# Fewer bank marks, a later third banded set and lean first-pass quads in a gated attention-and-mixer kernel

## The chip, the cores and the metric

One core of one Trainium2 chip. The metric is the device time of one execution, in microseconds (us), and lower is better. A kernel is compared only with the runs of the kernel before in the same rounds on the same chip.

## The reference, cut to what matters

Two branches work on the same x (2048 rows of 1024 columns), and a gate mixes them.

```python
g = sigmoid((x * gate_w).sum(-1, keepdims=True))
# a: attention over 8 positions, two apart (32 heads of 32)
qkv = x @ wqkv                               # banded q.k products, softmax over 8, weighted sum of v
a = o @ wo
# b: gated mixer
z = gelu(x @ w_in)                           # z1: 1792 columns, z2: 1792 columns
z2 = layernorm(z2)
b = (z1 * (w_sp @ z2 + b_sp)) @ w_out
out = g * a + (1 - g) * b
```

## The kernel before

TensorE does all products. Most large ones are done in "quads": a Strassen-like scheme that makes four output blocks from seven products instead of eight. A quad uses four PSUM banks, X, Y, Z and V. Its intermediate sums stay in PSUM: a copy or an addition by another engine puts one bank's content into another, and the next product adds onto it. Two quads run interleaved, one on banks 0 to 3 and one on banks 4 to 7.

```python
def chain(..., put, share, N, lean=False, ...):      # the quad of z2 and z1
    X, Y, Z, V = bank_roles[side]
    bank_roles[side] = [X, V, Y, Z] if lean else [Y, V, X, Z]
    product(X, pairs(A11, B11), True, N)
    last_seed[0] = nc.scalar.copy(Y[:, n], X[:, n])
    yield
    product(V, pairs(S1, T1), True, N)               # share: vs <- V
    ...
    product(Y, pairs(S2, T2), False, N)
    plus(Z, Y)                                       # VectorE: Z = Y + vs
    yield
    product(X, pairs(A12, B21), False, N)
    put(0, 0, X)                                     # ScalarE: gelu
    yield
    product(Y, pairs(S3, T3), False, N)
    if not lean:
        seed = nc.scalar.copy(X[:, n], Y[:, n])      # a bank of its own for the last block
    inst = plus(V, Y)
    if not lean:                                     # one reader of a bank at a time
        tc.add_manual_dep(inst.ins, seed.ins.name, SYNC, ...)
    put(1, 1, V)
    yield
    product(Z, pairs(S4, B22), False, N)
    put(0, 1, Z)
    yield
    W = Y if lean else X
    product(W, pairs(A22, T4), False, N)
    put(1, 0, W)
```

The kernel is built on the rule that a product adds onto what another engine wrote only where an earlier product has marked the bank. The kernel makes such marks with products whose results are thrown away:

```python
def mark(bs, N=512, lo=0):
    for b in bs:
        pe((N - lo) / 2400.0)                        # the planner's clock, see below
        nc.tensor.matmul(b[:, lo:N], xT[:, 4, 0:P], xT[:, 4, 0:N - lo], start=(lo == 0), stop=True, ...)
```

The attention's q.k products ("banded sets", three for each of eight groups of heads) use banks 4 to 7 as well. ScalarE casts each set into a staging buffer, and transfers store it from there to DRAM. The first set of a group has a buffer of its own, the second and third share two in turn. Later transfers load the sets back, rearranged, as the logits that VectorE works on.

```python
def group_tiles(g):                                  # the order of TensorE's work in group g
    ...                                              # tiles: the q and k products of the next group
    return [tiles[0], band[0], tiles[1], band[1], tiles[2], band[2]] + tiles[3:]
```

Between 60 and 280 us the order of VectorE's attention work and of all transfers is not written down. A planner decides it while the program is built: it keeps a modelled clock for each engine (`pe(dur)`, `act(...)`, `dve(...)`) and issues a transfer or an attention operation when its turn comes on those clocks. In this stretch the transfers go out on one queue, SP's, in that order.

```python
play(main[0:8 - (not g)])
if g == 2:                                           # the v quads, in the middle of group 2
    mark(banks[4:8])
    for i in range(0, 8, 2):
        run(v_quad(i), v_quad(i + 1), step=step)     # step: let the planner issue what is due
...
mark(banks[4:8], ZC)                                 # before the z2 quads (ZC = 448 columns)
...
mark(banks, 512, ZC)                                 # before z1, the columns 448 to 511
```

The z2 quads run in two passes; only the second is lean (`LEAN = (False, True)`).

## Time and profile before

673.67 us, median of three runs (673.57 to 673.83).

From the page of the kernel before, its first two parts' totals and the chain of waits by engine:

```profile
span 673.4 us, 10760 instructions
## 1 busy us (share of the span) xinstructions
PE 661.3 (98%) x4193; PEld 316.9 (47%) x4193; DVE 449.8 (67%) x663; ACT 296.8 (44%) x627; POOL 6.9 (1%) x15
...
PE 86%; ACT 5%; DVE 5%; DMA 2%; issue 1%; SPq 0%; POOL 0%; ACTq 0%; DVEq 0%
```

PE (TensorE) is the bound. What it can lose is gaps between products, and products that compute nothing. The timeline of TensorE alone shows both. Its columns are start, duration, engine, line, operation and shapes, the count, and in brackets the idle time before and what ended it. L288 are q and k tiles, L350 banded sets, L576 marks, L808 z2 tiles, L431 the products of quads.

```profile
83.14 0.64 PE L350 MATMUL psum_all<-arena 32*64 32x71 bf16 x56 [0.23 <-ACT arena L358]
...
87.18 1.03 PE L576 MATMUL psum_all<-arena 128*128 128x512 bf16 x4
88.05 30.59 PE L431 MATMUL psum_all<-arena 128*128 128x320 bf16 x224
118.67 7.07 PE L288 MATMUL psum_all<-arena 128*128 128x512 bf16 x32
...
162.00 0.64 PE L350 MATMUL psum_all<-arena 32*64 32x71 bf16 x56 [0.47 <-ACT arena L358]
...
195.96 0.92 PE L576 MATMUL psum_all<-arena 128*128 128x448 bf16 x4 [0.38 <-ACT arena L358]
196.72 12.41 PE L431 MATMUL psum_all<-arena 128*128 128x448 bf16 x64
209.38 1.67 PE L431 MATMUL psum_all<-arena 128*128 128x448 f16 x8 [0.25 <-ACT arena L801]
211.39 3.19 PE L431 MATMUL psum_all<-arena 128*128 128x448 f16 x16 [0.33 <-ACT psum_all L504]
214.94 3.94 PE L431 MATMUL psum_all<-arena 128*128 128x448 f16 x20 [0.36 <-DVE psum_all L492]
219.29 7.05 PE L431 MATMUL psum_all<-arena 128*128 128x448 bf16 x36 [0.40 <-ACT psum_all L526]
226.89 11.07 PE L431 MATMUL psum_all<-arena 128*128 128x448 f16 x56 [0.55 <-DVE psum_all L492]
238.27 42.58 PE L431 MATMUL psum_all<-arena 128*128 128x448 f16 x220 [0.31 <-DVE psum_all L492]
280.68 0.19 PE L576 MATMUL psum_all<-arena 128*128 128x64 bf16 x1
281.64 0.36 PE L576 MATMUL psum_all<-arena 128*128 128x64 bf16 x7 [0.77 <-ACT arena L801]
281.84 252.98 PE L431 MATMUL psum_all<-arena 128*128 128x512 bf16 x1168
535.03 135.10 PE L431 MATMUL psum_all<-arena 128*128 128x512 f16 x624 [0.21 <-DVE arena L1123]
```

Read it from the top: banded sets wait for ScalarE's cast of the set before (L358); three places carry marks (L576); the first z2 pass (196.7 to 238.3 us) has six gaps, the second pass (to 280.7 us) none that is listed; and from 282 us TensorE runs without a listed gap to the output stage at 535 us.

### The profile page before, as it was taken

Reading aid. Unit: us, or ns where it says so; the run is one execution under the profiler, and the core shown is the slowest. Engines: PE = TensorE matmul, PEld = TensorE weight load, DVE = VectorE, ACT = ScalarE, POOL = GpSimd, SP = SyncE. Lnnn points to the kernel's source line nnn. Section 1 sums busy time; section 2 is a strip of 40 time slices with the busy share of each in tenths; the row PEclk is TensorE's granted clock in tenths of the full one; section 3 lists DMA queues with packets and bytes.
Section 4 is the critical chain, followed back from the end, with each engine's and each line's share of the span. In section 5 each row is a group of like instructions: output and inputs, shape, how many; then the busy total and the mean of one; then the engine's idle time right before and its main releaser. Section 6 shows DMA issues by size and latency. Waiting matters only on the chain.

```text
span 673.4 us, 10760 instructions
## 1 busy us (share of the span) xinstructions
PE 661.3 (98%) x4193; PEld 316.9 (47%) x4193; DVE 449.8 (67%) x663; ACT 296.8 (44%) x627; POOL 6.9 (1%) x15
## 2 busy tenths in 40 slices
PE   8999999999999999999999999999999999999998
PEld 4544467444444445444444444444444444444443
DVE  2520699957997999897679676887766685333301
ACT  3354676556578767697854212112112112222221
POOL 1000000000000000001000000000000000000000
PEclk9999999999999999999999999999999999999999
DMA  9988554777476041359983477557356398954100
GB/s 228 167 209 225 116 121 125 210 193 198 95 200 175 1 125 29 94 149 219 234 211 134 99 174 175 139 146 235 102 139 167 87 192 189 202 121 101 44 31 32
DMA packets 235684, 98.17 MB, mean 146 GB/s; under 512 B 189792, under 2 KB 221936, under 8 KB 235632
## 3 DMA queue, kind: packets, MB, share of 16 engines
q1 hardware_dynamic: 234944, 97.01, 59.2%
q8 instruction: 33, 0.54, 0.4%
q10 hardware_dynamic: 688, 0.46, 0.2%
q14 instruction: 19, 0.16, 0.1%
HBM read 45.10 MB, written 36.61 MB: 121 GB/s over the span
## 4 chain that ended last, share of the span: by engine, by line
PE 86%; ACT 5%; DVE 5%; DMA 2%; issue 1%; SPq 0%; POOL 0%; ACTq 0%; DVEq 0%
PE psum_all L431 67%; PE psum_all L288 14%; PE psum_all L298 3%; ACT arena L358 2%; PE psum_all L350 1%; DVE psum_all L492 1%; ACT arena L801 1%; DMA band_d<-arena 1%; DVE arena L977 1%; DMA att_L<-band_d 1%; DVE arena L698 1%; PE psum_all L313 1%; DMA arena<-o_d 0%; PE psum_all L576 0%; ACT arena L291 0%
## 5 line engine op out<-in xcount | busy, mean ns | idle before, releaser
L431 PE MATMUL psum_all<-arena 128*128 128x512 f16 (+5 forms) x2436 | 500.1, 367 | 2.9 <-DVE psum_all L492 1.2
L431 PEld LDWEIGHTS <-arena 128*128 128x128 f16 (+1 forms) x2436 | 238.2, 98 | 264.2 <-issue 7.9
L288 PE MATMUL psum_all<-arena 128*128 128x512 bf16 x512 | 114.9, 379 | 0.9 <-ACT gl_s L301 0.8
L288 PEld LDWEIGHTS <-arena 128*128 128x128 bf16 x512 | 48.5, 98 | 57.7 <-issue 2.1
L694 DVE TENSOR_TENSOR arena<-arena,att_A 128x2048 f16<-128x2048 bf16 (+1 forms) x44 | 73.5, 1704 | 0.3
L291 ACT CAST arena<-psum_all 128x512 bf16<-128x512 f32 x64 | 37.3, 586 | 49.2 <-PE psum_all L288 49.2
L567 DVE TENSOR_TENSOR arena<-arena 128x1024 f16<-128x1024 f16 (+3 forms) x36 | 20.6, 582 | 47.6 <-PE psum_all L431 26.7
L449 ACT COPY psum_all<-psum_all 128x512 f32<-128x512 f32 (+1 forms) x30 | 15.8, 527 | 79.0 <-PE psum_all L431 78.2
L492 DVE TENSOR_TENSOR psum_all<-psum_all,arena 128x448 f32<-128x448 f32 (+1 forms) x58 | 37.2, 660 | 9.1 <-PE psum_all L431 5.2
L801 ACT ACTIVATE arena<-psum_all 128x448 bf16<-128x448 f32 x64 | 34.1, 546 | 19.1 <-DVE psum_all L492 11.2
L569 DVE TENSOR_TENSOR arena<-arena 128x1024 f16<-128x1024 f16 (+3 forms) x36 | 20.6, 580 | 29.3 <-PE psum_all L431 12.5
L1044 ACT ACTIVATE arena<-psum_all 128x512 bf16<-128x512 f32 x56 | 30.9, 595 | 18.2 <-PE psum_all L431 12.1
L698 DVE TENSOR_TENSOR arena<-arena 128x2048 f16<-128x2048 f16 (+1 forms) x22 | 37.2, 1703 | 0.1
L470 ACT COPY psum_all<-psum_all 128x512 f32<-128x512 f32 (+1 forms) x30 | 15.9, 529 | 46.2 <-PE psum_all L431 45.1
L358 ACT CAST arena<-psum_all 128x1988 f16<-128x1988 f32 (+3 forms) x25 | 33.9, 1357 | 5.0 <-DMA band_d<-arena 2.5
L460 ACT COPY psum_all<-psum_all 128x512 f32<-128x512 f32 (+1 forms) x30 | 15.7, 527 | 40.5 <-PE psum_all L431 40.0
L455 ACT COPY arena<-psum_all 128x512 f32<-128x512 f32 (+1 forms) x30 | 16.2, 543 | 35.3 <-PE psum_all L431 30.2
L851 ACT ACTIVATE arena<-arena 128x896 bf16<-128x896 bf16 x32 | 30.0, 943 | 0.0
L568 DVE TENSOR_TENSOR arena<-arena 128x1024 f16<-128x1024 f16 (+3 forms) x36 | 20.6, 582 | 8.2 <-PE psum_all L431 7.9
L1230 DVE TENSOR_TENSOR arena<-psum_all,arena 128x512 bf16<-128x512 f32 x8 | 5.5, 690 | 29.0 <-ACT psum_all L470 29.0
L298 PE MATMUL psum_all<-arena 128*128 128x385 bf16 x128 | 22.6, 327 | 0.3 <-DVE arena L321 0.3
L657 DVE TENSOR_TENSOR att_m<-att_L 128x256 f16<-128x256 f16 x8 | 2.3, 288 | 29.4 <-DMA att_L<-band_d 29.3
(89 smaller groups left out, 414.0 us busy)
## 6 DMA issues: line engine op xcount, KB each, us to landing
arena<-v_d SPq DMA_DIRECT2D x8, 960.0 KB, 6.5
z_d<-arena SPq DMA_DIRECT2D x14, 512.0 KB, 3.7
arena<-z_d SPq DMA_DIRECT2D x14, 512.0 KB, 4.3
zg_d<-arena SPq DMA_DIRECT2D x56, 128.0 KB, 2.2
arena<-zg_d SPq DMA_DIRECT2D x32, 224.0 KB, 3.1
band_d<-arena SPq DMA_DIRECT2D x28, 248.5 KB, 4.7
arena<-in_A_wqkv_dram SPq DMA_DIRECT2D x16, 256.0 KB, 4.4
o_d<-arena SPq DMA_DIRECT2D x4, 1024.0 KB, 6.1
```

The lines of the kernel that those rows point to most:

```text
L288: nc.tensor.matmul(ps[:], w[:, t, kt, :], xT[:, kt, 512 * c:512 * (c + 1)], start=(kt == 0), stop=(kt == KT - 1))
L291: nc.scalar.copy(dst[:, :, 256 * c:256 * (c + 1)], ps[:].rearrange("p (n e) -> p e n", e=2))
L298: nc.tensor.matmul(ps[:, 0:VP + 1], xT[:, kt, i * P:(i + 1) * P], wvp[:, kt, :], start=(kt == 0), stop=(kt == KT - 1))
L358: nc.scalar.copy(dst, src)
L431: nc.tensor.matmul(bank[:, 0:N], lhsT, rhs, start=(start and m == 0), stop=(m == n - 1), skip_group_check=True)
L492: last_add[0] = nc.vector.tensor_tensor(out[:, n], a[:, n], vs, ALU.add)
L567: first = nc.vector.tensor_tensor(s_out[0], a21, a22, ALU.add)
L694: lambda ws=ws, in0=in0, in1=in1: tt(p5[:, ws], in0[:, ws], in1[:, ws], ALU.mult)), False
L698: lambda a=p3[:, ws], b=p3[:, ws.start + 4:ws.stop + 4]: tt(a, a, b, ALU.add)), not n
L801: nc.scalar.activation(z2[:, i + 8 * a, ZC * c:ZC * (c + 1)], bank[:, 0:ZC], ACT.Gelu_apprx_tanh, accum_out=s1[:, 4 * n + c:4 * n + c + 1])
L851: return nc.scalar.activation(junk, src, ACT.Square, accum_out=(s2, s2h)[x][:, n:n + 1])
L1044: last_gelu[0] = nc.scalar.activation(z1s[:, f, a, :], bank[:], ACT.Gelu_apprx_tanh)
```

## The change

Its intent is to take small gaps and empty products from TensorE. Three parts:

- *Lean.* In the first z2 pass too, the last block is added onto Y, so the copy from Y to X and its ordering are not needed.
- *Bands.* The third banded set of a group comes one tile later, so that the cast of the second has two tiles' time.
- *Marks.* Only the banks that a quad needs marked (Y and Z; X and V are started afresh) are marked, and later, behind the quad's first product. At z1 the Y banks are still marked ahead of it, and the Z banks before the third products.

```diff
-    LEAN = (False, True)
+    LEAN = (True, True)
@@ group_tiles
+        if g + 1 < NG:
+            return [tiles[0], band[0], tiles[1], band[1], tiles[2], tiles[3], band[2]] + tiles[4:]
         return [tiles[0], band[0], tiles[1], band[1], tiles[2], band[2]] + tiles[3:]
@@ behind_first(n): at the first step of a pair of quads, mark(banks[5:7], n)   (cut)
@@ before the v quads
-            mark(banks[4:8])
             for i in range(0, 8, 2):
-                run(v_quad(i), v_quad(i + 1), step=step)
+                run(v_quad(i), v_quad(i + 1), step=behind_first(VH) if i == 0 else step)
@@ before the z2 quads
-    mark(banks[4:8], ZC)
@@ quad_step
+            if n == 0 and count[0] == 0:
+                mark(banks[5:7], ZC)
@@ before z1
-    mark(banks, 512, ZC)
+    mark([b[1] for b in bank_roles], 512, ZC)
@@ in the first pair of z1 quads, before its third products
+    mark([b[2] for b in bank_roles], 512, ZC)     # (simplified)
```

## The prediction

> **What bounds it now.** TensorE. On the page PE is 661.3 of 673.4 us (98%); the chain of waits is 86% PE; the granted clock is 1.00. The Trainium skill, "Perfetto Trace Analysis", section "Identifying the Most-Contended Engine", warns that matmul busy share does not show distance to roofline, so I count what PE can lose: gaps, and matmuls that compute nothing. PE's busy time per stretch shows about 12 us of gaps, 3 at startup and 3 at the end, both untouched; from 300 to 600 us under 0.5 us. So the change works between 60 and 300 us, where VectorE (DVE) is mostly over 90% busy.
>
> **What the change does.**
>
> 1. *Third banded set a tile later* (six groups, not the last). The banded products reuse four banks that ScalarE empties in 1.81 us after a 0.58 us tile copy; one tile of 1.72 us does not cover that. The timeline shows waits for that cast of 0.23, 0.47 and 0.29 us at 83, 162 and 178 us and 0.10 and 0.14 elsewhere. Two tiles cover it: -1.2 us. The 0.35 us at 193 stays.
> 2. *Marks.* Before the v quads four 512-wide matmuls become two of 320: 0.85 to 0.27 us, -0.6. Before the z2 quads four of 448 become two, behind the first product: -0.37, and most of a 0.38 us wait for the last banded cast goes: -0.7 in all. At z1 eight 64-wide ones become two and two, and the 0.77 us wait for a gelu at 280.7 goes, since the banks marked first are emptied earlier: -0.9. (Copies by VectorE and ScalarE do not set the bits that make a matmul add: "PSUM — Partial Sum Buffer", "The four PSUM rules"; no trace here shows the bits.)
> 3. *Lean z2 quads in the first pass.* Seven ScalarE copies of 0.54 us go, and with them 2.9 us of DVE waits for them. The last product now waits for DVE's addition, three products (2.3 us) behind. Between 196.7 and 238.3 us PE has 2.2 us of gaps (0.25 gelu, 0.33 seed copy, 0.40 removed copy, and 0.36, 0.55, 0.31 for additions); the second pass, already lean, has none over 0.2. I expect 1.4 back.
>
> **What comes back.** DVE is nearly full from 196 to 300 us and its work does not shrink. The instruction order shows two attention operations of 1.22 us pushed behind z1's start; PE may lead by that plus recovered DVE idle time. In the second quad pair DVE still sits behind the load of the last group's logits (1.94 us idle at 205). I allow 0.8 us of new waits there or in early z1.
>
> **Sum.** 1.2 + 0.6 + 0.7 + 0.9 + 1.4 - 0.8 = 4.0 us on PE's critical path: 673.67 to 669.6 us. Range 668.2 to 671.8. Faster by over 2%: 1%; within 2%: 98%; slower by over 2%: 1%.
>
> **What would show it.** No wait for the banded cast before the last group; z2 quads start about 2.5 us earlier; gaps in the first z2 pass fall from 2.2 to about 1; z1 starts about 4 us earlier with no gelu wait; after 300 us the lead stays constant. Wrong: PE's waits for additions grow, or the lead shrinks after 300 us.
>
> **What would make it wrong.** DVE's order comes from a planner with modelled clocks; if additions sit behind a 2.28 us attention operation or the logits' load, PE waits at the last product of a lean quad and up to 2 us come back.

## The result

670.95 us, median of four runs (669.78 to 672.09), against 673.69 us (673.57 to 673.83, four runs). The ratio is 0.9959, with a 95% interval of 0.9935 to 0.9983. The four runs fall into two pairs, 669.8 and 672.05 us, with granted clocks of 0.997 to 1.000; the profile is of one of the faster pair.

The page of the changed kernel:

```profile
span 668.0 us, 10729 instructions
...
PE 657.8 (98%) x4185; PEld 315.7 (47%) x4185; DVE 448.9 (67%) x663; ACT 293.1 (44%) x620; POOL 6.8 (1%) x15
...
PE 88%; DVE 7%; DMA 2%; SPq 1%; issue 1%; ACT 0%; DVEq 0%
```

TensorE is busy 3.5 us less and the span is 5.4 us shorter. ScalarE's share of the chain has gone from 5% to nothing, and VectorE's has grown from 5 to 7%. The removed copies explain little of that: in the chain before, the casts of the banded sets (L358) are 2.5%, the gelus (L801) 1.3%, and the removed copies (L526) 1.3 us, or 0.2%. SPq is the sequencer that issues the transfers, and it is now 1% of the chain.

The timeline of TensorE alone of the changed kernel, in the same columns as before:

```profile
85.89 0.71 PE L431 MATMUL psum_all<-arena 128*128 128x320 bf16 x4
86.43 0.43 PE L576 MATMUL psum_all<-arena 128*128 128x320 bf16 x2
86.70 30.05 PE L431 MATMUL psum_all<-arena 128*128 128x320 bf16 x220
116.78 7.07 PE L288 MATMUL psum_all<-arena 128*128 128x512 bf16 x32
...
157.10 0.64 PE L350 MATMUL psum_all<-arena 32*64 32x71 bf16 x56 [0.25 <-ACT arena L358]
...
161.80 0.64 PE L350 MATMUL psum_all<-arena 32*64 32x71 bf16 x56 [0.50 <-ACT arena L358]
...
193.87 0.54 PE L576 MATMUL psum_all<-arena 128*128 128x448 bf16 x2
194.25 5.46 PE L431 MATMUL psum_all<-arena 128*128 128x448 bf16 x28
200.39 71.61 PE L431 MATMUL psum_all<-arena 128*128 128x448 f16 x376 [0.69 <-DVE psum_all L492]
272.23 2.58 PE L431 MATMUL psum_all<-arena 128*128 128x448 f16 x12 [0.23 <-DVE psum_all L492]
274.65 0.22 PE L576 MATMUL psum_all<-arena 128*128 128x64 bf16 x2
274.71 3.62 PE L431 MATMUL psum_all<-arena 128*128 128x512 bf16 x16
...
306.55 221.63 PE L431 MATMUL psum_all<-arena 128*128 128x512 f16 x1024 [0.54 <-DVE psum_all L492]
529.59 135.10 PE L431 MATMUL psum_all<-arena 128*128 128x512 f16 x624 [1.41 <-DVE arena L1136]
```

The marks are smaller and sit behind the first products, as intended, and the gelu wait at z1 is gone. The first z2 pass has one gap left instead of six. But two waits for the banded cast are still there, at 157 and 162 us, and three waits later on are new or larger: 0.23 us at the end of the second z2 pass (272.2), 0.54 us at 306.6 and 1.41 us at the output stage (529.6, before 0.21).

The lead of the changed kernel at the same point of TensorE's program, worked out from such lines of the two timelines (start before minus start after):

| point | lead, us | gained in the stage | predicted |
|---|---|---|---|
| q and k tiles at 48.0 us, ahead of all changed code | 0.8 | 0.8 | 0 |
| end of the v quads (118.67, 116.78) | 1.9 | 1.1 | 1.8 for the bands and these marks, |
| ahead of the z2 quads | 2.3 | 0.4 | these two rows together |
| behind the z2 marks | 3.2 | 0.9 | 0.7 |
| z1 marks (280.68, 274.65) | 6.0 | 2.8 | 1.4 |
| z1's products behind them (281.84, 274.71) | 7.1 | 1.1 | 0.9 |
| output stage (535.03, 529.59) | 5.4 | -1.7 | -0.8 somewhere |
| end of the span (673.4, 668.0) | 5.4 | 0 | 0 |

This table is of one of the faster executions, which is 3.9 us below the median of before; the median gain of all four is 2.7 us. So the predicted total held, but it was not made up of the predicted terms. The first 0.8 us is chance: no instruction ahead of that point differs. The z2 passes gave twice what was predicted. The bands and the first marks gave 1.5 of 1.8, and 1.7 us was lost late.

*Why the z2 passes gave more.* The gaps listed in a TensorE timeline are too short, because a matmul's record is longer than the matmul's spacing. In the changed kernel 376 matmuls of 448 columns took 71.61 us, that is 0.1905 us each (0.190 from start to start, as the 71.61 includes the last record's overhang), while their records average 352 ns. The last record ahead of a stall therefore covers about 0.16 us of it. From start to start the account is different. Before, the six stretches from 196.72 to 238.27 us hold 200 matmuls in 41.55 us. They need 38.10, so 3.45 us were lost, while the listed gaps add up to 2.20. After, 28 matmuls take 6.14 us from 194.25 to 200.39 and need 5.33, so 0.81 was lost, and no gap is listed behind that in this pass. The difference is 2.64 us, against 1.51 by listed gaps (2.20 less 0.69).

### The profile page after: what moved, and what is told of

Same layout as the page of the kernel before. It is cut to its first block, busy times and chain, and to the rows that moved or that the text cites. A ratio compares the mean times of both kernels' runs of the same rounds, so it can differ in the third digit from the quotient of the medians.

```text
span 668.0 us, 10729 instructions
## 1 busy us (share of the span) xinstructions
PE 657.8 (98%) x4185; PEld 315.7 (47%) x4185; DVE 448.9 (67%) x663; ACT 293.1 (44%) x620; POOL 6.8 (1%) x15
## 4 chain that ended last, share of the span: by engine, by line
PE 88%; DVE 7%; DMA 2%; SPq 1%; issue 1%; ACT 0%; DVEq 0%
PE psum_all L431 71%; PE psum_all L288 12%; PE psum_all L298 3%; DVE arena L694 3%; DMA band_d<-arena 1%; PE psum_all L350 1%; DVE arena L698 1%; SPq L186 1%; PE psum_all L313 1%; DMA arena<-o_d 1%; DVE arena L699 1%; DVE psum_all L492 0%; DVE arena L703 0%; DMA att_L<-band_d 0%; ACT arena L300 0%
## 5 line engine op out<-in xcount | busy, mean ns | idle before, releaser
L567 DVE TENSOR_TENSOR arena<-arena 128x1024 f16<-128x1024 f16 (+3 forms) x36 | 20.7, 584 | 53.4 <-PE psum_all L431 26.7
L801 ACT ACTIVATE arena<-psum_all 128x448 bf16<-128x448 f32 x64 | 34.1, 545 | 19.8 <-DVE psum_all L492 10.8
L569 DVE TENSOR_TENSOR arena<-arena 128x1024 f16<-128x1024 f16 (+3 forms) x36 | 20.6, 582 | 26.8 <-PE psum_all L431 12.1
L358 ACT CAST arena<-psum_all 128x1988 f16<-128x1988 f32 (+3 forms) x25 | 33.9, 1356 | 4.8 <-DMA band_d<-arena 2.7
L568 DVE TENSOR_TENSOR arena<-arena 128x1024 f16<-128x1024 f16 (+3 forms) x36 | 20.6, 583 | 8.1 <-PE psum_all L431 7.9
L570 DVE TENSOR_TENSOR arena<-arena 128x1024 f16<-128x1024 f16 (+3 forms) x36 | 20.4, 580 | 1.7 <-PE psum_all L431 1.6
```

The source lines that it names most:

```text
L358: nc.scalar.copy(dst, src)
L567: first = nc.vector.tensor_tensor(s_out[0], a21, a22, ALU.add)
L801: nc.scalar.activation(z2[:, i + 8 * a, ZC * c:ZC * (c + 1)], bank[:, 0:ZC], ACT.Gelu_apprx_tanh, accum_out=s1[:, 4 * n + c:4 * n + c + 1])
```

## The experiments

The texts name theories by letters. P is the prediction's account, in which the parts have the worths that can be read in the trace. D is its rival in the first set, in which the changed kernel has two levels of time. S, formed after the first set, and O in the third set hold that the order in which the planner issues its work decides. Twelve runs were made in three sets, each set on one chip of its own. All twelve gave correct results. The medians of the kernel before in the same rounds were 674.63 us (673.26 to 675.90) in set 1, 674.85 (673.77 to 676.80) in set 2 and 675.44 (673.64 to 676.91) in set 3.

| run | set | median us (range) | ratio to before [95%] | waits for the banded cast, us |
|---|---|---|---|---|
| a1_again: the changed kernel | 1 | 671.23 (668.61-673.23) | 0.9949 [0.9927, 0.9971] | 1.0 |
| l1_lean_only | 1 | 671.79 (671.31-672.36) | 0.9957 [0.9943, 0.9971] | 1.5 |
| b1_bands_only | 1 | 673.06 (672.54-677.46) | 0.9986 [0.9963, 1.0009] | 0 |
| m1_marks_only | 1 | 676.05 (673.55-677.63) | 1.0017 [0.9998, 1.0036] | 4.3 |
| m2_marks_clock_kept | 2 | 673.15 (672.62-674.26) | 0.9970 [0.9955, 0.9985] | 0.4 |
| u1_after_no_bands | 2 | 671.82 (670.79-673.22) | 0.9954 [0.9937, 0.9971] | 2.4 |
| k1_after_clock_kept | 2 | 668.64 (668.60-669.56) | 0.9909 [0.9894, 0.9924] | 0 |
| b0_before_again: one profile | 2 | 674.24, state unknown | - | 1.0 |
| a2_third: the changed kernel | 3 | 672.60 (670.54-673.47) | 0.9958 [0.9941, 0.9974] | 2.3 |
| k3_kept_no_bands | 3 | 671.54 (670.67-675.69) | 0.9960 [0.9936, 0.9984] | 1.3 |
| k4_kept_no_lean | 3 | 672.07 (670.66-673.65) | 0.9953 [0.9937, 0.9970] | 0 |
| k2_kept_late_sums | 3 | 669.27 (667.95-670.80) | 0.9910 [0.9893, 0.9926] | 0 |

The last column is what the view of waits of each run's one profile gives for TensorE's listed waits for the cast at L358 between 60 and 186 us; waits too short for that view are not in it. In the profiles of before and after it is 1.0 and 0.7.

### Set 1: the parts alone

**The changed kernel again.** No edit.

> The changed kernel again. Its four times lay at 669.8 and 672.05, two each. Theory D: the 2.2 us between them come from when transfers land (the load of the last stage's first rows, for which the changed kernel waited 1.4 us at 529.6 us even in its fast profile, or the stores of the bands at 154 to 162 us); then the new runs fall at the same two levels, about half each, and never between. Rival C: a matter of the chip; then all runs of one chip fall at one level. Granted clock stays 0.997 to 1.00 either way.

It ran from 668.6 to 673.2 us. That is neither one level nor two: the two pairs of the first result were chance, and D's two levels fall. On this chip the kernel before spreads by 2.6 us as well.

**Lean alone.**

```diff
-    LEAN = (False, True)
+    LEAN = (True, True)
```

> Only the lean quads. Theory P (the parts add up as read from the trace of after, where the lead over the kernel before grew by 2.7 to 2.8 us in the z2 passes): 2 to 2.8 us faster than before, 670.9 to 671.7. Rival M (removed waits move to the next reuse of a bank, only all parts together pay): under 1 us faster. Gaps of PE between 196.7 and 238 us fall from 2.2 to under 1 us.

It is 0.43% faster, 2.9 us of 674.63 (2.0 to 3.8 by the interval). That agrees with the account from start to start (2.64) and not with the predicted 1.4. Its profile keeps one gap in the first pass, 0.96 us for an addition at 207.70 us, ahead of the last product of a lean quad, where the prediction looked for one.

**Bands alone.** Only the new branch of `group_tiles`.

```diff
+        if g + 1 < NG:
+            return [tiles[0], band[0], tiles[1], band[1], tiles[2], tiles[3], band[2]] + tiles[4:]
```

> Only the third banded set a tile later. Theory P: the lead of after grew 0.9 us over the six groups, so 0.5 to 1.0 us faster, 672.7 to 673.2. Rival M: same as before within 0.3 us, the later bands being paid back in the attention's chain or at the marks before the v quads.

It is 0.14% faster, 0.9 us, and the interval includes no gain at all. Its profile has no wait for the cast up to 186 us. Two tiles do cover the cast, here.

**Marks alone.** The whole third part, without the other two.

```diff
-            mark(banks[4:8])
-                run(v_quad(i), v_quad(i + 1), step=step)
+                run(v_quad(i), v_quad(i + 1), step=behind_first(VH) if i == 0 else step)
-    mark(banks[4:8], ZC)
+            if n == 0 and count[0] == 0:
+                mark(banks[5:7], ZC)
-    mark(banks, 512, ZC)
+    mark([b[1] for b in bank_roles], 512, ZC)     # and b[2] later, as in the change
```

> Only the marks. Theory P: 0.6 at the v quads, 0.7 to 0.9 at z2, 0.9 to 1.1 at z1, together 2.0 to 2.6 us faster, 671.1 to 671.7. Rival M: only the 1.0 us of matmuls removed, 672.7.

Both theories missed this. TensorE has less to do, and the kernel is not faster; the measured ratio is 1.0017. From TensorE's timeline of this run, the second 56-matmul banded set of three successive groups:

```profile
145.47 0.64 PE L350 MATMUL psum_all<-arena 32*64 32x71 bf16 x56 [0.73 <-ACT arena L358]
...
162.73 0.64 PE L350 MATMUL psum_all<-arena 32*64 32x71 bf16 x56 [1.70 <-ACT arena L358]
...
179.69 0.64 PE L350 MATMUL psum_all<-arena 32*64 32x71 bf16 x56 [1.41 <-ACT arena L358]
```

In the profile of before no wait at these sets was over 0.47 us. And from the timeline of all engines of the same run, the cast that the middle one waits for:

```profile
160.86 1.82 ACT L358 CAST arena<-psum_all 128x1988 f16<-128x1988 f32 x1 [1.62 <-DMA band_d<-arena]
```

The cast is no longer than before (1.82 us), but ScalarE stood idle for 1.62 us ahead of it, waiting for a transfer: the store that empties the staging buffer the cast writes into. So the bound at this place is not ScalarE's time, as the prediction had it, but when the stores of the banded sets come due and land.

What had changed for them? A mark calls `pe(...)`, so a smaller mark also advances the planner's modelled clock by less. Around the v quads that is 4 x 512 - 2 x 320 = 1408 columns at 2400 a microsecond: 0.587 us. The planner then issues transfers and VectorE's work in another order. This is theory S.

### Set 2: the clock kept

**Marks alone, with the planner's clock as before.**

```diff
+            pe(4 * 512 / 2400.0 - 2 * VH / 2400.0)   # ahead of the v quads; no instruction
+    pe(2 * ZC / 2400.0)                              # ahead of the z2 quads
```

> The marks alone again, TensorE's instructions as in the marks-only kernel (which came out 0.17% slower than before), but the planner's clock is advanced by what the removed marks took, so that up to z1 the transfers and VectorE's work are issued in the order of the kernel before. Theory S (the marks are worth 2.0 to 2.6 us; the marks-only kernel lost them because the shifted planner reordered the stores of the bands among the weight loads, and ScalarE's casts, and then TensorE, waited for those stores: 3.8 us of waits at 145, 163 and 180 us): 1.5 to 2.5 us faster than before, and the three waits are back at 0.1, 0.5 and 0.3 us. Rival W (marks are worth nothing, whatever comes earlier waits at the next reuse): within 0.5 us of before or slower, as marks-only was.

TensorE's instructions are the same as in the marks-only kernel. Up to z1, transfers and VectorE's work stand in the order of the kernel before. It is 0.30% faster than before, 2.0 us, and its interval does not touch that of marks alone. The predicted 2.2 us for the marks was right, but only with the order kept.

**The changed kernel without the bands.**

```diff
-        if g + 1 < NG:
-            return [tiles[0], band[0], tiles[1], band[1], tiles[2], tiles[3], band[2]] + tiles[4:]
```

> The changed kernel with the third banded set back in its old place (lean quads and marks kept). Theory S: the move of the set is also what shields TensorE from late stores of the bands, so undoing it costs 2.5 to 4 us against the changed kernel (waits for the cast of 0.7 to 1.7 us in the groups from 140 to 180 us return): about 0 to 1.5 us faster than before. Rival A (parts simply add): undoing it costs the 0.9 us that bands-only gained, so 2.0 to 2.5 us faster than before.

I had expected that the later third set is what shields the changed kernel from the reordered stores, so that this one would gain only 0 to 1.5 us. It gained 0.46%, 3.1 us, about as much as the changed kernel itself. The waits for the cast did grow, to 2.4 us, but the time did not show it. The shield as I had it is not borne out. In the profiles, this kernel lacks what the later set brings further on (the waits at 272.2 and 306.6, see the end of Set 3), and its wait at the output stage is 0.19 instead of 1.41 us.

**The changed kernel with the planner's clock kept.** One line, ahead of the v quads; TensorE's instructions are unchanged.

```diff
+            pe(4 * 512 / 2400.0 - 2 * VH / 2400.0)
             for i in range(0, 8, 2):
```

> The changed kernel with the planner's clock advanced at the v quads as above; the transfers of groups 3 to 6 are then ordered as in bands-only, whose profile shows no wait for the cast there. Theory S: the waits of 0.25 and 0.50 us (0.97 us in the second profile of after) at 157 to 163 us go, 0.7 to 1.2 us faster than the changed kernel, 0.6 to 0.7% faster than before. Rival: those waits stay, being a matter of when the memory serves the stores, and the time is that of the changed kernel.

It is 0.91% faster than before, 6.1 us: more than either theory expected, so the waits at 157 to 163 us are not all that the order cost. The three ratios of the changed kernel are 0.9949, 0.9958 and 0.9959, and no interval of these reaches down to this one's upper end of 0.9924. So the changed kernel loses 0.40 to 0.50% to the order, 2.7 to 3.4 us. A sum check: lean alone (2.9), bands alone (0.9) and marks with the clock kept (2.0) make 5.8 us.

The cost of the order is shown in two pairs of kernels with the same instructions on TensorE: this one (0.40 to 0.50%) and marks alone without and with the clock kept (0.47%). A third pair does not show it: the changed kernel without the bands is at 0.9954 without and, in Set 3, at 0.9960 with the clock kept. The intervals leave room for a gain of about 0.23% at most there.

From the timeline of the changed kernel, issues on the transfer queue (SPq) and VectorE's first operation on the loaded logits:

```profile
128.79 0.60 SPq L186 DMA_DIRECT2D o_d<-arena  x1
129.44 2.03 SPq L186 DMA_DIRECT2D arena<-v_d  x1
...
148.20 1.28 SPq L186 DMA_DIRECT2D att_L<-band_d  x2
...
152.87 0.29 DVE L657 TENSOR_TENSOR att_m<-att_L 128x256 f16<-128x256 f16 x1 [8.15 <-DMA att_L<-band_d]
```

And from the same view of the changed kernel with the clock kept:

```profile
124.25 0.61 SPq L186 DMA_DIRECT2D o_d<-arena  x1
...
129.60 0.58 SPq L186 DMA_DIRECT2D arena<-v_d  x1
...
145.10 1.28 SPq L186 DMA_DIRECT2D att_L<-band_d  x2
...
149.75 0.29 DVE L657 TENSOR_TENSOR att_m<-att_L 128x256 f16<-128x256 f16 x1 [7.84 <-DMA att_L<-band_d]
```

The same logits are asked for 3.1 us later in the changed kernel, although its v quads had started 0.3 us earlier (85.89 against 86.17). The store of o has moved behind two stores of banded sets and two weight loads. The load of v keeps its place and its time. In this profile the chain of waits of the changed kernel leads from there to TensorE's remaining gap; its columns are start, duration and what ran:

```profile
154.35 7.28 DMA band_d<-arena
161.65 2.44 DMA att_L<-band_d
...
197.51 2.28 DVE arena L694
199.79 0.56 DVE psum_all L492
200.39 5.64 PE psum_all L431 x29
```

A store of a banded set takes 7.28 us to land, the load of the logits follows it, VectorE works through its attention operations without a break of note, and the addition that TensorE waits for at 200.39 comes at their end. With the clock kept, TensorE's timeline has no gap in this pass:

```profile
193.66 76.83 PE L431 MATMUL psum_all<-arena 128*128 128x448 bf16 x404
```

That does not show that the order makes this gap, however. In the kernel of Set 3 with late sums, whose transfers and VectorE's work stand in the order of the kernel with the clock kept up to 520 us, the gap is there:

```profile
200.91 71.61 PE L431 MATMUL psum_all<-arena 128*128 128x448 f16 x376 [0.65 <-DVE psum_all L492]
```

And the changed kernel's third profile has none. The gap at this product stands in seven of the ten profiles with new marks (0.65 to 1.35 us) and in none of the four with the old ones, lean or not. So it goes with the new marks rather than with the order; how it comes about is not shown.

The two profiles differ by 1.2 us at the end only (668.0 and 666.8), since the changed kernel was profiled in one of its faster executions.

**The kernel before, one look.**

> The kernel before, profiled again, to see what moves from run to run without any change. Expected: the waits that begin with a transfer (first block of x, stores of the bands, rows of the last stage) differ by up to 1 us from its first profile; waits between engines alone (seeds, additions, gelus) are the same to 0.1 us.

Most of its waits repeat those of the first profile: 1.0 us for the cast, 0.18 us at the output stage, and four of the six gaps of the first z2 pass to 0.01 us. The other two, 0.25 us for a gelu and 0.33 us for a seed copy, are gone, so not all waits between engines are the same to 0.1 us. Up to the last of these gaps the pass takes 40.71 us here against 41.55, so the account from start to start carries that much chance.

### Set 3: what the order costs, and to whom

**The changed kernel a third time.** No edit.

> The changed kernel a third time, to stand on one chip beside the clock-kept variants below. Theory O (the planner's order of transfers is what the changed kernel loses against its clock-kept sister): 0.4 to 0.6% faster than before, its profile again with waits of 0.7 to 1 us for the cast between 150 and 165 us and 0.7 to 1.4 us for the first additions of the z2 quads. Rival H (the 0.91% of the clock-kept kernel was the chip's doing): 0.8 to 0.9% here too.

The ratio repeats. The profile caught a slower execution (672.95 us), with one wait of 2.34 us for the cast at 164.02, behind a cast that stood idle 4.01 us for the store of a banded set. The view by stretches of this run shows what it cost beyond itself; its columns are the stretch, its length, the busy time of PE, PEld, DVE, ACT and POOL with counts, the granted TensorE clock, the DMA share and GB/s:

```profile
164.00:166.00 2.00, 1.98 (x60) 1.08 (x60) 0.83 (x1) 2.00 (x3) 0.00 (x0) 0.50 0.73 92
166.00:168.00 2.00, 2.00 (x8) 0.81 (x7) 1.63 (x5) 1.12 (x2) 0.00 (x0) 0.67 0.81 189
168.00:170.00 2.00, 2.00 (x11) 0.91 (x10) 1.97 (x3) 1.01 (x3) 0.00 (x0) 1.00 0.84 222
```

The granted clock was 0.50 in the 2 us behind the stall and 0.67 in the mean of the next 2. The 40 tile products that follow took 10.09 us, against 8.81 in the faster profile. So a stall of 2.34 us cost about 3.6. Such a stall can account for part of the spread of the changed kernel's times. No wait for an addition in z2 came with it, which the expectation had named.

**The clock kept, without the bands.** Against the changed kernel:

```diff
+            pe(4 * 512 / 2400.0 - 2 * VH / 2400.0)
-        if g + 1 < NG:
-            return [tiles[0], band[0], tiles[1], band[1], tiles[2], tiles[3], band[2]] + tiles[4:]
```

> Lean quads and marks with the clock kept, the third banded set in its old place. Theory O with parts that add once the order is right (lean 2.9, marks 2.0, bands 0.9 us alone): 4.5 to 5.2 us faster than before, 0.67 to 0.77%. If instead the later set is the main shield against late stores, under 3.5 us faster, with waits over 0.7 us for the cast in the groups from 140 to 180 us.

It gained 0.40%, 2.7 us, less than expected, and 0.51% less than with the bands. So the bands are worth 3.4 us here and 0.9 alone. By the table's intervals these are 1.5 to 5.3 and -0.6 to 2.5 us, which overlap, so it is not shown that the parts fail to add; two of this kernel's six runs (673.42 and 675.69) pull its mean up. The waits in one profile (1.3 us) do not explain 3.4 us.

**The clock kept, the first pass not lean.** Against the changed kernel:

```diff
+            pe(4 * 512 / 2400.0 - 2 * VH / 2400.0)
-    LEAN = (True, True)
+    LEAN = (False, True)
```

> Bands and marks with the clock kept, the first z2 pass not lean. Adding parts: 2.7 to 3.5 us faster than before (0.40 to 0.52%), and the first z2 pass shows waits for the removed copies and the additions again, 1.5 to 2.3 us of them between the start of the z2 quads and the second pass. If lean is worth only the 1.4 us predicted, 4.5 us or more faster.

It gained 0.47%, as expected. The lean part is worth 0.44% here, 3.0 us, the same as alone.

**The clock kept, and the output stage's first sums behind the last addition of the spatial quads.** This was aimed at the wait of 1.41 us at the output stage. Against the changed kernel with the clock kept:

```diff
+            first = sums4(...)                       # the attention-row part of output quad 0
+            if i == 0 and k0:
+                tc.add_manual_dep(first.ins, wait_for[0].ins.name, NOSYNC, ...)
```

> The clock-kept kernel, with the sums for the first output quad that wait for the attention's rows placed behind the last spatial quad's additions on VectorE (the scheduler also moves some of TensorE's products there). If the wait at the start of the output stage (0.5 to 1.5 us at 528 to 530 us in four of six profiles of kernels with new marks) is these sums standing ahead of the additions while their transfer is under way: that wait falls under 0.3 us and the kernel is 0.5 to 1.3 us faster than the clock-kept one's 0.91%. If the transfer itself gates the products: same time, the wait moved to the sums' own product.

Inconclusive. The ratio is 0.9910, as without the edit, on another chip. (On this chip the changed kernel stands at 0.9958, so the gain of the kept clock is seen on one chip too.) In its profile the wait is gone, but the transfer that feeds those sums was not late in that profile, so the edit had nothing to mend; another wait of 0.62 us stood in its place.

Across all profiles that wait goes with the time that the issue of o's transposing loads takes: waits of about 0.2 us where it was 12.20 to 12.28 us, 0.4 to 0.5 where it was 12.33 to 12.41, 1.4 to 1.7 where it was 12.60 or more. With the old marks it was never over 0.25 us (four profiles); with the new ones it was 0.39 to 1.66 in eight of nine, this last kernel aside. So it goes with the new marks, though no run shows how. The kernel with the clock kept has it too (1.49 us) and is still the fastest.

**The fourteen profiles together.** Some kernels issue transfers and VectorE's work in the same order up to the z2 quads, so their profiles can be pooled (labels shortened). TensorE's listed waits for the cast up to 186 us were:

| third banded set | order | profiles | waits, us |
|---|---|---|---|
| old place | of before | before, b0, l1, m2, k3 | 0.4 to 1.5 |
| old place | shifted by the marks | m1, u1 | 4.3, 2.4 |
| a tile later | as in bands alone | b1, k1, k2, k4 | 0 |
| a tile later | shifted by the marks | after, a1, a2 | 0.7, 1.0, 2.3 |

So two tiles cover the cast in the one order and not in the other. The z2 passes, from their first product to the z1 marks, took 83.0 to 84.4 us in the six profiles whose first pass is not lean and 80.6 to 82.2 us in the eight where it is, 2.35 us less in the mean. And the later set has a price: all seven profiles with it have the wait of 0.23 us just before z1 and one of 0.50 to 0.55 us some 30 us into z1. Of the seven without it, only marks alone has a similar one (0.30 us, in z1).

## Why the prediction was right or wrong

The total was right: 669.6 us predicted, 670.95 measured, inside the range. It was right because errors cancelled.

- *TensorE bounds, and the work lies between 60 and 300 us:* right. With TensorE's program held fixed, however, the time still moved by about 3 us in two of three pairs of kernels, so what releases TensorE mattered as much as its own program.
- *Lean, 1.4 us:* right mechanism, mis-sized. It measured 2.9 us alone and 3.0 in the kernel with the clock kept. Two other pairs in the table give 4.2 (marks alone against the changed kernel without bands) and 0.7 (the same two with the clock kept), each uncertain by about 1.8 us. The listed gaps did fall by about what was predicted, 1.51 us, but the term should have been built from start to start, where they came to 2.64 us: each listed gap of before understates its stall, by 0.2 us in the mean (1.25 us over six).
- *Marks, 0.6 + 0.7 + 0.9 = 2.2 us:* right as a price of TensorE's instructions (2.0 us with the order kept). On top of lean, with the clock kept, they added nothing (0.9960 against 0.9957, uncertain by 1.9 us). Alone they gave nothing (1.0017), because smaller marks advance the planner's clock by 0.59 us less and its order shifts.
- *Bands, 1.2 us, and "No wait for the banded cast before the last group":* this step failed. Alone the move gave 0.9 us, with an interval that includes no gain, and no waits for the cast; but in the changed kernel 0.7 to 2.3 us of waits stayed. "Two tiles cover it" took the cast's 1.81 us as the bound. The runs showed that the cast itself waits for the store of its staging buffer, and so for the order of the transfers.
- *What comes back, 0.8 us:* mis-sized, and for another reason than named. The changed kernel gives back 2.7 to 3.4 us against the one with the clock kept. The prediction looked for VectorE work pushed behind z1's start; the runs show transfers and VectorE's work reordered from the v quads on. The risk named at the end did occur, as the 0.69 us wait at 200 us: the addition stands right behind "a 2.28 us attention operation". But it came in the first pair of quads, at the fifth product and not the last, and it comes without lean quads too (0.65 us in marks with the clock kept).
- *"z2 quads start about 2.5 us earlier; gaps in the first z2 pass fall from 2.2 to about 1":* the lead there was 2.3 us, 0.8 of it chance, and the gaps fell to 0.69. Both about right.
- *"z1 starts about 4 us earlier with no gelu wait":* 6.0 us, of which 0.8 us is chance; the gelu wait is gone.
- *"after 300 us the lead stays constant":* wrong by 1.7 us, from the waits at 306.6 and 529.6 us. The first comes at an addition and goes with the later banded set; the second goes with the new marks, varies from run to run with a transfer, and also stands in kernels of equal or better time. Both of the prediction's own signs for "wrong" showed, this one and growing waits for additions (1.2 to 1.5 us listed over the whole run), although the total was right.

What stays open: how the loss of about 3 us divides between the order of transfers and that of VectorE's work, which shift together with the planner's clock; why keeping the clock gains nothing without the bands; whether the bands are worth more with the clock kept (3.4 us) than alone (0.9); and what makes the output stage's transfer late in some executions.

## What to carry to other kernels

Price a stall of TensorE from start to start of its products, against the spacing of an unbroken stretch, not by the idle time listed. Where a planner with modelled clocks orders a shared transfer queue, a change that moves those clocks by half a microsecond can reorder it and cost as much as one part of the change saves, as it did in two of three pairs here: compare the order of transfers before and after, and separate the two by an experiment that keeps the clock and changes the instructions only.

## What the Trainium skill lacked or had wrong

- "TensorE: Matmul & The Clock Gate", section "Back-to-back issue gap", gives about 131 ns as the sustained spacing for 512 columns, and calls its formula N/2.4 + 2.5 an over-count there. Here 1024 such products took 221.63 us, 216 ns each, which is what the formula gives (215.8). For 448 columns it gives 189.2, and about 190 was measured.
- The same page, section "HAM oscillation — how this bites in real kernels", states as the abstract rule that idle gaps should not exceed about 3.4 us. In the third run of the changed kernel a gap listed as 2.34 us was followed by a granted clock of 0.50 for 2 us and 0.67 in the mean of 2 more.
- "PSUM — Partial Sum Buffer", section "Summary: rules for kernel authors", says that a seed written by VectorE or ScalarE must be 0. These kernels seed with non-zero sums behind one marking product, and all twelve runs were correct, also those that mark two banks of four. The page's own section "The four PSUM rules" (it adds where the bit is set) agrees with them; no trace shows the bits.
- "Perfetto Trace Analysis", section "Identifying the Most-Contended Engine", says that pipelined TensorE instructions look smaller in the trace. Here records are longer than the spacing (352 against 190.5 ns for 448 columns), so that listed gaps are short by about 0.16 us each. Its section "Summary: the profiler window per engine type" calls the end of a TensorE record estimated, which agrees.
- I found no page that says what the order of issue on one queue costs when independent transfers share it. Here a shifted order of transfers, and of VectorE's work with it, was worth 0.40 to 0.50% of the time in two pairs of kernels and nothing measurable in a third.
